# The attention's output stage on TensorE: state products of a tile first, then its value products

## The chip, the cores and the metric

The kernel runs on one core of one Trainium2 chip. The metric is device time in microseconds (us) of one launch: 959.07 us is the median of three runs of the kernel before. One further execution was taken with the hardware profiler; every row below is from that one.

## The reference

Three stages follow one another. The first is a linear attention with a decay per key dimension, over 4 batches, 8 heads, 768 steps and a head dimension of 48:

```python
for t in range(S):
    state = f[:, :, t, :, None] * state + einsum('bhd,bhe->bhde', k[:, :, t], v[:, :, t])
    y[:, :, t] = einsum('bhd,bhde->bhe', q[:, :, t], state)
```

Its output, as 3072 rows of 384, goes through a dense layer (`x @ w_in`, softplus, `@ w_out`, with 2048 hidden columns), and that result through eight experts of 1024 hidden columns. Each expert takes 384 rows, assigned greedily by the gate's logits. All of it is in fp32.

## The kernel before

**The attention in tiles.** The 768 steps of a batch are cut into 6 tiles of 128 steps, 24 tiles in all. `wide_attention(g)` computes one. It brings the keys and queries of all 8 heads into decayed form (`kb`, L363, and `qb`, L367; two heads, a *pair*, share the 128 rows of a PSUM column block), multiplies them to the masked score matrix `A` (L372, L374), carries the state on into the next tile (`kt` by L380, state sum by L386, L393 and L394), and then makes the output `py`. `py` is one PSUM bank of 128 steps x 8 heads x 48 columns.

**The output stage, L396 to L403.** Two kinds of matmul add up in `py`, all in fp32:

- the *state product* of a pair, L399: stationary `qb[:, pr, :]` (128 columns), moving `s_old[:, pr, :]` (96 columns), output on all 128 partitions. A tile has four of them. The first tile of a batch has no old state and leaves them out, so 20 of the 24 tiles have them.
- the *value products*, L402: for each head and each half `z` of the 128 steps the stationary operand is `A[:, h, z]` (64 columns), the moving one is `vn[:, h, :]` (48 columns), and the output is on 64 partitions. A tile has sixteen.

Before the change the four pairs go one after another: the state product of the pair, then the four value products of its two heads. Each state product carries `start=True`; the value products of these tiles carry `start=False` and add to it. In a batch's first tile the value products carry `start=True`.

In the trace each of these fp32 matmuls shows as two records, so a state product is "x2" and the four value products of a pair are "x8".

**What comes after it.** `finish` (L311) copies `py` to `x` on ScalarE (L313), transposes it on TensorE (L320) and splits it into `xh` (L322) and `xl` (L323), the input of the dense layer `moe1`. `moe1(u)` takes three tiles at a time. Per block `fc` of 128 hidden columns it runs nine matmuls into `h` (L558), then ScalarE (L561 to L563), VectorE (L564, L569) and GpSimd (L570, `gl`) make the softplus and split it in two parts, and up to nine matmuls into `acc` use them (L502 and L503 with `gh`, L504 with `gl`).

**What sets the order.** The streams (weights in, attention tiles, dense layer) are merged step by step in `merge`, and a scheduler that simulates the engines' time then fixes the order of instructions on each engine. TensorE executes its list in that order. Code written in another order thus moves the two loops of the output stage, and may also move what the scheduler puts around them, on every engine. From the expert stage on, TensorE's order is written by hand.

In the early part, the weights of the dense layer come as 64-bit numbers and VectorE decodes them to fp32 tiles `w` (L444 to L446); TensorE transposes some of them (L467), ScalarE copies that out (L469, `wT`), and TensorE multiplies it by the gate (L473).

Of the kernel before, what the change touches and what calls it, by code (L numbers as in the profile page):

```python
# [73 lines left out]
def body(ctx, tc, q, k, v, f_logit, w_in, w_out, w_gate, w1, w2, c_mask, c_mat, out, wide):  # L74
    nc = tc.nc
    B, H, S, D = q.shape
    DM = H * D
    NP = H // 2
# [85 lines left out]
    def to_T(x, early=False):  # L164
        p = ps_h.tile([128, NP, 128], F32, name="h") if early else ps_at.tile([128, NP, 128], F32, name="p_at")
        for pr in range(NP):
            nc.tensor.transpose(p[:, pr, :], x[:, 2 * pr:2 * pr + 2, :].rearrange("p a d -> p (a d)"), ident)  # L167
        return p
# [142 lines left out]
    def finish(g, py):  # L311
        x = att.tile([128, DM], F32, name="x", bufs=1)
        nc.scalar.activation(x, py.rearrange("p h d -> p (h d)"), AF.Copy)  # L313
        u, j = divmod(g, TU)
        if j == 0:
            XT[u] = [(xtc() if wide is not None and u > 2 and u % 3 == 1 else xtp).tile([128, DC, TU * 128], F32R, name=n) for n in ("xh", "xl")]
        xh, xl = XT[u]
        px = ps_at.tile([128, DC, 128], F32, name="p_at")
        for c in range(DC):
            nc.tensor.transpose(px[:, c, :], x[:, c * 128:(c + 1) * 128], ident)  # L320
        js = slice(j * 128, (j + 1) * 128)
        nc.scalar.activation(xh[:, :, js], px, AF.Copy)  # L322
        nc.vector.tensor_sub(xl[:, :, js], px, xh[:, :, js].bitcast(F32))  # L323
# [27 lines left out]
    def wide_attention(g):  # L351
        b, i = divmod(g, S // 128)
        first, last = i == 0, i == S // 128 - 1
        qn, kn, vn = loaded.pop(g)
        G, R = decays.pop(g)
        A = AA[g % NF]
        half = (slice(0, 64), slice(64, 128))
        mul = nc.vector.tensor_mul
        pair = lambda x, pr: x[:, 2 * pr:2 * pr + 2, :].rearrange("p a d -> p (a d)")

        pk = to_T(kn, g < GA)
        kb = att.tile([128, NP, 128], F32, name="kb")
        mul(kb, pk, G)  # L363
        yield
        pq = to_T(qn, g < GA)
        qb = att.tile([128, NP, 128], F32, name="qb")
        mul(qb, pq, R)  # L367
        yield
        p = [ps_at.tile([128, NP, 128], F32, name="p_at") for _ in half]
        for pr in range(NP):  # L370
            for z, a in zip(half, p):
                nc.tensor.matmul(a[:, pr, :], kb[z, pr, :], qb[z, pr, :], start=True, stop=True)  # L372
        for r, a in enumerate(p):
            nc.vector.copy_predicated(A[:, r::2], mask[:, 0, None, :].to_broadcast([128, NP, 128]), a)  # L374
            yield
        s_old, s_new = SS[i % 2], SS[(i + 1) % 2]
        if not last:
            pt = ps_at.tile([128, NP, 128], F32, name="p_at")
            for pr in range(NP):
                nc.tensor.transpose(pt[:, pr, :], kb[:, pr, :], ident)  # L380
            kt = att.tile([128, NP, 128], F32, name="kt", bufs=1)
            nc.scalar.activation(kt, pt, AF.Copy)
            yield
            pS = ps_at.tile([128, NP, 2 * D], F32, name="p_at")
            for pr in range(NP):
                nc.tensor.matmul(pS[:, pr, :], kt[:, pr, :], pair(vn, pr), start=True, stop=True)  # L386
            for r in range(2):
                h, c = half[r], slice(D * r, D * r + D)
                end = R[h, :, 127:].to_broadcast([64, NP, D])
                if first:  # L390
                    mul(s_new[h, :, c], pS[h, :, c], end)
                else:
                    nc.vector.tensor_add(s_new[h, :, c], pS[h, :, c], s_old[h, :, c])  # L393
                    nc.gpsimd.tensor_mul(s_new[h, :, c], s_new[h, :, c], end)  # L394
            yield
        py = ps_at.tile([128, H, D], F32, name="p_at")  # L396
        for pr in range(NP):
            if not first:
                nc.tensor.matmul(pair(py, pr), qb[:, pr, :], s_old[:, pr, :], start=True, stop=False, skip_group_check=True)  # L399
            for h in (2 * pr, 2 * pr + 1):  # L400
                for z in half:
                    nc.tensor.matmul(py[z, h, :], A[:, h, z], vn[:, h, :], start=first, stop=True, skip_group_check=True)  # L402
        finish(g, py)  # L403
        yield

# [246 lines left out]
    for g in range(NU * TU):  # L652
        if wide is None:
            streams.append((load_f(g), g * 30.0 - 9.1, 30.0, 1))
            streams.append((load_tile(g), g * 30.0 - 9.0, 30.0, 1))
            streams.append((counted(attention(g), left_t), g * 30.0, 60.0, 26))
        else:
            t = g * TA if g < NA else NA * TA + (g - NA) * TB
            streams.append((load_f(g), t - TF - TA, TA, 1))
            streams.append((decay(g), t - TF, DD, 4))  # L660
            streams.append((load_tile(g), t - TA, TA, 1))
            streams.append((counted(wide_attention(g), left_t), t, TD, 8) + ((AH,) if g < NH else ()))
# [76 lines left out]
    if fast:  # L739
# [4 lines left out]
        first = cst.tile([128, KF], F32, name="first")  # L744
# [551 lines left out]
```

## Time and profile before

| | |
|---|---|
| three runs | 958.22, 959.07 and 961.91 us; median 959.07 us |
| the profiled execution's own time | 963.57 us |
| its span, first to last instruction | 961.8 us |
| TensorE busy | 902.9 us, 94% of the span, 6605 matmul records |
| VectorE, ScalarE, GpSimd busy | 498.0, 469.2 and 480.7 us |
| mean granted TensorE clock | 0.966 of full speed |

The profiled execution is 4.50 us above the median. An engine's busy time is the sum of its instructions' durations with overlaps counted once. Matmuls are pipelined, so one matmul's duration is longer than the distance to the next; the distance from start to start is what a matmul costs in a row of them. In the timeline's rows the first number is the start in us from the span's beginning, the second the time from the first start to the last end of the merged records. A bracket at the end of a row names how long the engine sat idle before it and who released it.

### The profile page before, as it was taken

To read this page: it belongs to the slowest core of one execution; us is meant where nothing else is said; L and a number is where in the kernel's file an instruction comes from. 1 tells how busy PE (TensorE), PEld (TensorE's weight loads), DVE (VectorE), ACT (ScalarE), POOL (GpSimd) and SP (SyncE) were. 2 spreads that over 40 slices of the span, in tenths; PEclk is the share of its full clock that TensorE was granted. 3 is DMA by queue.
4 is the path that set the end of the run, shared out by engine and by line. 5 is a ranking of instruction groups with operands and counts; after the bars stand their busy time and mean duration, and the time that the engine had idled before them with its cause. 6 is when DMAs were issued, how large, how long until landed. Compare 5 with 4: busy or idle time off the path is not lost.

```text
span 961.8 us, 17212 instructions
## 1 busy us (share of the span) xinstructions
PE 902.9 (94%) x6605; PEld 842.6 (88%) x6605; DVE 498.0 (52%) x1275; ACT 469.2 (49%) x959; POOL 480.7 (50%) x500
## 2 busy tenths in 40 slices
PE   3888999999999999999999999999699999999995
PEld 2778999999999999999999998889588889889895
DVE  6886887444445445544553343335465656652320
ACT  3565656455554555555545676733243334335321
POOL 6664665334534344543332443546565676558721
PEclk9977999999999999999999998999799999999898
DMA  9563341122222212222100000003144325427200
GB/s 174 157 172 91 95 119 34 50 42 47 63 42 43 58 36 48 49 56 38 26 25 2 25 1 10 1 17 139 43 157 157 118 88 178 160 66 247 75 26 29
DMA packets 130844, 72.20 MB, mean 75 GB/s; under 512 B 102464, under 2 KB 120256, under 8 KB 130752
## 3 DMA queue, kind: packets, MB, share of 16 engines
q1 hardware_dynamic: 77216, 52.04, 18.6%
q10 hardware_dynamic: 50464, 9.52, 5.8%
q0 software_dynamic: 3072, 9.44, 2.9%
q8 instruction: 54, 0.88, 0.4%
q14 instruction: 38, 0.31, 0.1%
HBM read 61.55 MB, written 9.44 MB: 74 GB/s over the span
## 4 chain that ended last, share of the span: by engine, by line
PE 79%; DVE 6%; issue 6%; ACT 3%; DMA 3%; POOL 3%; SPq 0%; ACTq 0%; POOLq 0%; DVEq 0%
PE h L558 20%; PE h L1170 7%; PE acc L502 7%; PE acc L504 6%; PE acc L503 6%; PE p_at L167 3%; PE p_at L402 3%; PE p_at L399 3%; PE acc L1159 3%; PE p_at L372 2%; PE acc L1161 2%; PE acc L1160 2%; PE p_at L386 2%; PE counts L1012 2%; PE counts L1080 1%
## 5 line engine op out<-in xcount | busy, mean ns | idle before, releaser
L570 POOL TENSOR_TENSOR g<-e,g 128x384 fp32r<-128x384 f32 x128 | 130.3, 1019 | 230.4 <-DVE g L569 223.9
L564 DVE SCALAR_TENSOR_TENSOR e<-h,e 128x384 f32<-128x384 f32 x123 | 68.1, 554 | 148.4 <-ACT e L563 147.8
L558 PE MATMUL h<-xh,wih 128*128 128x384 f32 x369 | 128.8, 350 | 1.5 <-DVE e L564 1.5
L558 PE MATMUL h<-xl,wih 128*128 128x384 f32 x369 | 126.8, 344 | 1.7 <-DVE xl L323 1.7
L558 PE MATMUL h<-xh,wil 128*128 128x384 f32 x369 | 127.0, 344 | 0.0
L561 ACT ACTIVATE e<-h 128x384 f32<-128x384 f32 x123 | 59.7, 486 | 111.8 <-PE h L558 109.4
L502 PE MATMUL acc<-woh,g 128*128 128x392 f32 x304 | 105.7, 351 | 0.6 <-DVE g L569 0.6
L503 PE MATMUL acc<-wol,g 128*128 128x392 f32 x304 | 104.0, 342 | 0.0
L504 PE MATMUL acc<-woh,g 128*128 128x392 f32 x304 | 86.8, 348 | 0.9 <-POOL g L570 0.9
L1123 POOL TENSOR_TENSOR w0l<-wf,w0h 128x512 fp32r<-128x512 f32 x48 | 61.2, 1305 | 43.4 <-ACT w0h L1120 41.0
L1176 ACT ACTIVATE hh<-h 128x384 fp32r<-128x384 f32 x64 | 31.0, 486 | 103.2 <-PE h L1170 98.1
L563 ACT ACTIVATE e<-e,chalf 128x384 f32<-128x384 f32 x128 | 78.6, 614 | 3.3 <-ACT e L562 0.3
L558 PEld LDWEIGHTS h<-xh,wih 128*128 128x128 f32 x369 | 70.5, 191 | 4.3 <-DVE e L564 2.6
L1170 PE MATMUL h<-gxh,w0h 128*128 128x384 f32 x192 | 70.5, 367 | 2.9 <-DVE hl L1177 1.7
L558 PEld LDWEIGHTS h<-xl,wih 128*128 128x128 f32 x369 | 70.8, 192 | 2.2 <-DVE xl L323 2.0
L558 PEld LDWEIGHTS h<-xh,wil 128*128 128x128 f32 x369 | 70.7, 192 | 0.2
L1177 DVE SCALAR_TENSOR_TENSOR hl<-h,hh 128x384 fp32r<-128x384 f32 x64 | 35.5, 555 | 67.1 <-ACT hh L1176 66.8
L1159 PE MATMUL acc<-w1h,hh 128*128 128x384 f32 x192 | 68.2, 355 | 0.0
L562 ACT ACTIVATE e<-e 128x384 f32<-128x384 f32 x128 | 66.8, 523 | 2.8 <-ACT e L561 0.3
L1170 PE MATMUL h<-gxl,w0h 128*128 128x384 f32 x192 | 66.8, 348 | 0.3 <-DVE gxl L1144 0.2
L569 DVE CAST g<-e 128x384 fp32r<-128x384 f32 x128 | 58.0, 455 | 17.3 <-PE acc L549 6.5
L1170 PE MATMUL h<-gxh,w0l 128*128 128x384 f32 x192 | 66.4, 346 | 0.0
(260 smaller groups left out, 2175.8 us busy)
## 6 DMA issues: line engine op xcount, KB each, us to landing
wf<-in_moe_w_dram SPq DMA_DIRECT2D x32, 768.0 KB, 7.2
raw<-in_moe_w_in_dram SPq DMA_DIRECT2D x16, 384.0 KB, 3.2
raw<-in_moe_w_out_dram SPq DMA_DIRECT2D x16, 384.0 KB, 3.1
natf<-in_f_logit_dram SPq DMA_DIRECT2D x24, 192.0 KB, 3.1
natk<-in_k_dram SPq DMA_DIRECT2D x24, 192.0 KB, 3.2
natq<-in_q_dram ACTq DMA_DIRECT2D x24, 192.0 KB, 3.6
vn<-in_v_dram ACTq DMA_DIRECT2D x24, 192.0 KB, 2.8
X<-x SPq DMA_DIRECT2D x24, 192.0 KB, 1.9
```

The lines of the kernel that those rows point to most:

```text
L502: nc.tensor.matmul(a, gh[:, js], woh[:, fc, :a.shape[1]], start=(fc == 0), stop=False)
L503: nc.tensor.matmul(a, gh[:, js], wol[:, fc, :a.shape[1]], start=False, stop=False)
L504: nc.tensor.matmul(a, gl[:, js], woh[:, fc, :a.shape[1]], start=False, stop=(fc == FB - 1))
L558: nc.tensor.matmul(h, w[:, c, fs], x[:, c, :], start=(n == 0), stop=(n == 3 * DC - 1))
L561: nc.scalar.activation(e, h, AF.Abs)
L562: nc.scalar.activation(e, e, AF.Exp, scale=-1.0)
L563: nc.scalar.activation(e, e, AF.Ln, bias=chalf, scale=0.5)
L564: nc.vector.scalar_tensor_tensor(e, h, 0.0, e, op0=OP.max, op1=OP.add)
L570: nc.gpsimd.tensor_sub(gl, e, gh.bitcast(F32))
L1123: nc.gpsimd.tensor_sub(l, src[:, c], h.bitcast(F32))
L1159: nc.tensor.matmul(acc[j], hh[:, js], bh[:, fc, :], start=(fc == 0), stop=False)
L1170: nc.tensor.matmul(h, w[:, c, fs], x[:, c, :], start=(n == 0), stop=(n == 3 * DC - 1))
```

## The change

The two loops are taken apart. All four state products of a tile are issued first, then all sixteen value products. Only the first state product carries `start=True`, the flag that clears the bank; the other three write other columns of the same bank without it. The number of matmuls, their operands and their shapes stay the same.

```diff
         py = ps_at.tile([128, H, D], F32, name="p_at")
-        for pr in range(NP):
-            if not first:
-                nc.tensor.matmul(pair(py, pr), qb[:, pr, :], s_old[:, pr, :], start=True, stop=False, skip_group_check=True)
-            for h in (2 * pr, 2 * pr + 1):
-                for z in half:
-                    nc.tensor.matmul(py[z, h, :], A[:, h, z], vn[:, h, :], start=first, stop=True, skip_group_check=True)
+        if not first:
+            for pr in range(NP):
+                nc.tensor.matmul(pair(py, pr), qb[:, pr, :], s_old[:, pr, :], start=(pr == 0), stop=False, skip_group_check=True)
+        for h in range(H):
+            for z in half:
+                nc.tensor.matmul(py[z, h, :], A[:, h, z], vn[:, h, :], start=first, stop=True, skip_group_check=True)
         finish(g, py)
         yield
```

What the scheduler makes of it stands in TensorE's and VectorE's lists. A tile in the middle of the program, on TensorE (`SS_107` is the old state, `AA_105` the scores, `g_3438` the softplus of one block of the dense layer); three more pairs of rows like the first two, all with a minus, stand right ahead of these:

```order
-L399 MATMUL p_at<-SS_107,qb 128x96
-L402 MATMUL p_at<-vn,AA_105 64x48 x4
-L558 MATMUL h<-xh,wil 128x384
+L399 MATMUL p_at<-SS_107,qb 128x96 x4
+L402 MATMUL p_at<-vn,AA_105 64x48 x16
 L502 MATMUL acc_2776<-woh,g_3438 128x392
 L503 MATMUL acc_2776<-wol,g_3438 128x392
```

The eight alternating rows have become two, and one matmul of the dense layer has moved from behind the block to a place ahead of it. Of the 20 tiles with a state, 16 have exactly these two rows with nothing between. In the first two tiles three L473 matmuls stand among the value products, as they did before; in one later tile three L558 do, and in the last tile dense-layer matmuls do.

Early in the program, on TensorE, where the dense layer's first block begins (`w_738` is a decoded weight tile). Before:

```order
L558 MATMUL h<-xh,wih 128x384
L558 MATMUL h<-xl,wih 128x384
L558 MATMUL h<-xh,wil 128x384
L467 MATMUL p_at<-ident,w_738 128x128 x3
L473 MATMUL p_at<-wg,wT 128x8 x3
L380 MATMUL p_at<-ident,kb 128x128 x4
```

and now:

```order
L372 MATMUL p_at<-qb,kb 128x128 x8
L558 MATMUL h<-xh,wih 128x384 x2
L467 MATMUL p_at<-ident,w_738 128x128 x3
L558 MATMUL h<-xl,wih 128x384
L558 MATMUL h<-xh,wil 128x384
L558 MATMUL h<-xh,wih 128x384
```

The transposes of `w_738` (L467) stood behind all eighteen matmuls of two blocks; now they stand behind the first two of them. On VectorE, the same place:

```order
 L475 TENSOR_TENSOR wol<-acc_719,woh 128x8
-L323 TENSOR_TENSOR xl<-p_at,xh 128x3x128
 L446 SCALAR_TENSOR_TENSOR w_738<-raw,w_738 128x384
+L323 TENSOR_TENSOR xl<-p_at,xh 128x3x128
+L374 COPY_PREDICATED AA_105<-mask,p_at 128x4x128 x2
 L444 TENSOR_SCALAR w_758<-wt 128x384
-L374 COPY_PREDICATED AA_105<-mask,p_at 128x4x128 x2
```

The last step of `w_738` (L446) now comes ahead of `xl` (L323) instead of behind it.

## Rows read from the trace of the kernel before

**Rows 1.** The page: busy times of the engines, and the chain that ended last.

```profile
PE 902.9 (94%) x6605; PEld 842.6 (88%) x6605; DVE 498.0 (52%) x1275; ACT 469.2 (49%) x959; POOL 480.7 (50%) x500
...
PE 79%; DVE 6%; issue 6%; ACT 3%; DMA 3%; POOL 3%; SPq 0%; ACTq 0%; POOLq 0%; DVEq 0%
```

**Rows 2.** Stretches: length; busy PE, PEld, DVE, ACT, POOL (instructions); TensorE clock; DMA; GB/s.

```profile
50.00:90.00 40.00, 34.50 (x209) 31.46 (x210) 29.57 (x60) 22.71 (x52) 22.50 (x24) 0.71 0.51 138
90.00:185.00 95.00, 94.28 (x707) 89.58 (x706) 69.10 (x127) 59.27 (x130) 47.99 (x49) 1.00 0.32 79
185.00:512.00 327.00, 327.00 (x2547) 309.77 (x2547) 159.38 (x329) 167.23 (x320) 136.84 (x150) 1.00 0.21 42
512.00:640.00 128.00, 122.76 (x695) 114.39 (x694) 47.82 (x113) 80.27 (x164) 54.22 (x58) 0.96 0.02 7
```

**Rows 3.** Timeline of TensorE: the output stage of one tile, start, length, what.

```profile
311.93 0.36 PE L399 MATMUL p_at<-SS,qb 128*128 128x96 f32 x2
...
312.59 0.46 PE L399 MATMUL p_at<-SS,qb 128*128 128x96 f32 x2
312.98 0.44 PE L402 MATMUL p_at<-vn,AA 128*64 128x48 f32 x8
313.35 0.46 PE L399 MATMUL p_at<-SS,qb 128*128 128x96 f32 x2
...
314.87 0.44 PE L558 MATMUL h<-xh,wil 128*128 128x384 f32 x1
315.15 0.34 PE L502 MATMUL acc<-woh,g 128*128 128x392 f32 x1
315.32 0.34 PE L503 MATMUL acc<-wol,g 128*128 128x392 f32 x1
```

**Rows 4.** Timeline of TensorE: a batch's first tile, state sum (L386), then value products.

```profile
405.80 1.03 PE L386 MATMUL p_at<-vn,kt 128*128 128x96 f32 x8
406.76 1.14 PE L402 MATMUL p_at<-vn,AA 128*64 128x48 f32 x32
407.83 0.44 PE L558 MATMUL h<-xh,wih 128*128 128x384 f32 x1
```

**Rows 5.** Instructions of L399 and L402: duration ns min/median/max, first and last start.

```profile
L399 PE MATMUL p_at<-SS,qb x160: 243/276/351, 46.2 to 505.5; 128*128 128x96 f32 x160
...
L402 PE MATMUL p_at<-vn,AA x768: 221/222/343, 31.9 to 505.9; 128*64 128x48 f32 x192
```

**Rows 6.** Timeline of TensorE: a tile whose state sum stands right ahead of its output stage.

```profile
486.59 1.03 PE L386 MATMUL p_at<-vn,kt 128*128 128x96 f32 x8
487.46 0.39 PE L399 MATMUL p_at<-SS,qb 128*128 128x96 f32 x2
...
490.42 0.45 PE L502 MATMUL acc<-woh,g 128*128 128x392 f32 x1
```

**Rows 7.** The chain that ended last, in order of time: start, length, what.

```profile
62.93 0.37 PE p_at L402 x8
...
122.77 0.47 issue
...
133.94 1.83 PE h L558 x9
```

**Rows 8.** Timeline, 71 to 80 us: waits of TensorE, and VectorE's last decoding step.

```profile
71.96 0.81 DVE L446 SCALAR_TENSOR_TENSOR w<-raw,w 128x384 int32<-128x384 int32 x1
72.10 0.45 PE L558 MATMUL h<-xl,wih 128*128 128x384 f32 x1 [1.71 <-DVE xl L323]
...
76.55 0.49 PE L467 MATMUL p_at<-ident,w 128*128 128x128 f32 x3
...
79.51 1.33 PE L473 MATMUL p_at<-wg,wT 128*128 128x8 f32 x6 [2.46 <-ACT wT L469]
```

**Rows 9.** The page's costliest groups: busy, mean ns of one, idle before.

```profile
L570 POOL TENSOR_TENSOR g<-e,g 128x384 fp32r<-128x384 f32 x128 | 130.3, 1019 | 230.4 <-DVE g L569 223.9
...
L504 PE MATMUL acc<-woh,g 128*128 128x392 f32 x304 | 86.8, 348 | 0.9 <-POOL g L570 0.9
```

## The prediction

> **What bounds the kernel now.** I read the page first. TensorE is busy for 94% of the span and makes 79% of the chain that ended last; no other engine passes 52% [rows 1]. Since such a share is a mean over stages, I then cut the span into stretches [rows 2]. From 185 to 512 us TensorE is busy for 327.00 of 327.00 us, and from 90 to 185 us for 94.28 of 95.00, both at a granted clock of 1.00, the 2.4 GHz level. In these 422 us nothing but TensorE's own list sets the time, and any us taken off that list moves everything behind it forward. From 50 to 90 us it is different: TensorE is busy for 34.50 of 40 us and the mean clock is 0.71, a mixture of the 2.4 and the 1.2 GHz level. There, what TensorE saves may turn into waiting. The output stage runs in all three stretches, from 46.2 to 505.9 us [rows 5].
>
> Next I looked at the timeline of one tile's output stage [rows 3]. It begins at 311.93 and the next foreign matmul starts at 314.87, so the stage costs 2.94 us. Inside it, a state product (two records) takes 312.98 - 312.59 = 0.39 us from start to start, and the four value products of a pair (eight records) 313.35 - 312.98 = 0.37 us. No wait stands anywhere in it. The question is whether 0.39 and 0.37 are what such matmuls cost, or what the alternation costs.
>
> A batch's first tile answers it, because there the same shapes run unmixed [rows 4]. The state sum L386 has the state product's shape (128 x 128 stationary, 96 moving, fp32): eight records from 405.80 to 406.76, 0.96 us with the turn to the value products in it. With no turn behind it, the same eight take 487.46 - 486.59 = 0.87 us [rows 6]: 0.109 us a record, so two cost 0.22 us, not 0.39. The 32 records of sixteen value products take 407.83 - 406.76 = 1.07 us, or 0.27 us for eight, not 0.37. So each change of the stationary shape, from 128 to 64 columns or back, leaves a gap. A pair has two changes and pays 0.76 - 0.22 - 0.27 = 0.27 us for them.
>
> **The change, part by part.**
>
> *The gaps.* Removed: three of the four alternations of each tile with a state. The count of such tiles is 160 records of L399 / 2 records / 4 pairs = 20 [rows 5]. The new list for a tile, four state products and then sixteen value products, has the shapes and the order of the first tile's row pair, so I price it by that: 0.96 + 1.07 = 2.03 us [rows 4], against 2.94 us [rows 3]. I take 2.94 - 2.03 = 0.91 us for a tile; three pairs of gaps, 3 x 0.27 = 0.81 us, say nearly the same from inside the stage. Where the state sum stands right ahead of the stage, which is so in seven tiles, the stage takes 490.42 - 487.46 = 2.96 us [rows 6]; I take 0.93 us there. One difference is unpriced by these rows: the first tile's value products clear, the new ones accumulate. The row of eight accumulating ones bounds that from above, since 0.37 us for eight contains two changes of shape [rows 3]; without the changes they can't be slower than that, and 4 x 0.37 = 1.48 us in place of 1.07 would leave a gain of 0.50 us a tile. From below nothing speaks for faster ones. I take 1.07, since it is the row of an unbroken run.
>
> *Which tiles count.* The chain that ended last passes through the tile at 62.52 (its value products stand in it at 62.93), and leaves TensorE from 122.77 to 133.94 for a chain over the other engines [rows 7]. So the tile at 125.58, inside that gap, gains nothing for the end: TensorE would only wait longer at 133.94. The tile at 46.15 isn't in the chain either. The other 18 are. That gives 7 x 0.93 + 11 x 0.91 = 16.5 us. If the other engines' cover of those two tiles were not there, 2 x 0.91 = 1.8 us more would be won.
>
> *The flag.* Three clearing flags of a tile vanish. A flag is a bit of an instruction that is issued anyway. I cost it at nothing; in the rows no record differs in a way that would fit a cost for it, and its bounds are inside those of the value products above.
>
> *The rest of TensorE's list.* The scheduler has moved other matmuls too. A change of kind costs its gap there as well: the first L558 behind a block takes 315.15 - 314.87 = 0.28 us against 0.17 us for the next matmul [rows 3]. In the new list there are four fewer places where the dense layer's matmuls follow small ones, 4 x 0.11 = 0.4 us.
>
> *The early part.* The transposes of `w_738` now stand ahead of sixteen matmuls, and `xl` behind the last decoding step. Before, TensorE waited 1.71 us for `xl`; that can grow by the step that now goes ahead, 0.81 us [rows 8]. In return L473, which waited 2.46 us for `wT`, can be served earlier, since `wT` comes from those transposes. The bounds are -0.8 and +2.5 us. As the clock also moves between its levels here and the stretch isn't bound by TensorE, I take 0 and keep the bounds; a clock that stays low longer can eat the same 2.5, so I use 2.5 on both sides.
>
> *Other engines.* They issue what they issued, in slightly other places. DMA issues are the same; early on, the key and the decay load of one tile each go ahead of one weight load on SP's queue, which I count to the early part's bounds. PSUM: `py` is held about 0.9 us less. ScalarE's copy L313 follows the last value product, as before.
>
> The sum is 16.5 + 0.4 = 16.9 us. The profiled execution, 963.57 us with its span of 961.8, would become 946.7. It lies 4.50 us above the median, so I take the sum from the median: 959.07 - 16.9 = **942.2 us**, 1.8% less.
>
> **The rivals.**
>
> *Value products held to their weight loads.* The state products run at 0.109 us a record [rows 6], and if that is the load of 128 columns, one of 64 would take 0.054. Then 32 would cost 1.74 us and not 1.07, the stage 2.70, and 18 tiles would give 18 x 0.24 = 4.3 us: 954.8 us. For it speaks only that 0.109 fits a load. Against it: 1.07 us for 32 [rows 4], and eight accumulating ones in 0.37 us, two changes included, where eight loads alone would be 0.43 [rows 3]. The Trainium skill, page "TensorE: Matmul & The Clock Gate", section "LDWEIGHTS (loading the stationary operand)", states this rule: the load takes the number of columns divided by 1.2, in ns. An estimate by that page's figures is 8 x 107 + 32 x 53 = 2.56 us a tile without any gap; the trace agrees for 128 columns and disagrees for 64. Chance 0.04.
>
> *Half given back.* In the gap from 122.77 to 133.94 the other engines were as tight as TensorE [rows 7]. Were they so at every second tile, nine tiles would count: 9 x 0.91 + 0.4 = 8.6 us, 950.5 us. For it: the 16.5 us come out of 460 us, in which every other engine gets less time. Against: VectorE, the busiest, has 159.38 of 327 us in the long stretch [rows 2]. Chance 0.08.
>
> *Slower: TensorE meets L504 before GpSimd is done.* In the new list L504 often stands right behind L503 of the same accumulator, where matmuls of the next block stood between. L504 needs GpSimd's `gl`, 1019 ns an instruction, and waited only 0.9 us in all before [rows 9]. A late `gl` costs up to 1.02 us; to lose 0.5% (4.8 us) on top of the gain, (16.9 + 4.8) / 1.02, or 21 such waits in full, are needed. For it: the moves are many, among 85 blocks. Against: the scheduler moved L504 behind a simulated time of `gl`, and with the same rule it left two short waits before. It would give 964 us or more. Chance 0.03.
>
> *No difference.* That the change doesn't do what it says is ruled out by the list: 16 of 20 tiles have the two rows unbroken and the others nearly so. What remains is that the gap belongs to something that the new order keeps, such as adding to columns just written. Against: the turn back from value to state products writes other columns and leaves a gap too, since 0.39 and 0.37 are both too long. 959 us, chance 0.02.
>
> **How the numbers follow.** My forecast, 937 to 950, has a chance of 0.83. Its low end is all 20 tiles and the early bound, 16.9 + 1.8 + 2.5 = 21.2 us, or 937.9, and about 1 us for the runs' scatter. Its high end is the upper bound of the value block, 18 x 0.50 + 0.4 = 9.4 us, or 949.7. The range reaches on to the half given back, to 951; the cases above that hold less than 0.1. A measurement of this kernel can tell about 0.5%, 4.8 us, from no change. Faster by more than that: 0.83 + 0.08 = 0.91. Within it: 0.04 + 0.02 = 0.06. Slower: 0.03.
>
> **What would show it.** In the profile after, eight records of L399 should run from start to start of the value products in 0.96 us and 32 of L402 in about 1.07, the stage in 2.0 to 2.1 us. The record count stays 6605 but for lost ones, TensorE's busy time falls by 16 to 18 us, and the last output stage starts some 16 us before 505. The forecast is wrong if the value products stay at 0.37 us for eight, if new idle time of TensorE appears between 90 and 512 us, or if the long stretch gets shorter and a stretch behind it longer.

## The result, and the profile after

The changed kernel takes **943.14 us** (median of four runs, 941.18 to 946.80) against 958.64 us of the kernel before on the same chip (956.42 to 961.91): a ratio of 0.9847, 95% interval 0.9821 to 0.9874, or 15.5 us less. The prediction said 942.2 us, 937 to 951. The profiled execution took 942.85 us with a span of 941.0 us.

The page after, busy times and the chain that ended last, answers to [rows 1]:

```profile
PE 873.9 (93%) x6605; PEld 823.2 (87%) x6605; DVE 500.4 (53%) x1275; ACT 467.3 (50%) x959; POOL 482.9 (51%) x500
...
PE 77%; DVE 7%; issue 6%; ACT 3%; POOL 3%; DMA 3%; ACTq 0%; SPq 0%; POOLq 0%; DVEq 0%
```

The record count is the same and TensorE's busy time is 29.0 us less, while the span of the profiled execution fell by 20.8. So TensorE's idle time rose by 8.2 us, from 961.8 - 902.9 = 58.9 to 941.0 - 873.9 = 67.1. VectorE's share of the chain rises from 6% to 7%; it comes back below.

The same stretches as [rows 2], of the kernel after:

```profile
50.00:90.00 40.00, 34.13 (x238) 31.60 (x239) 33.78 (x63) 24.70 (x55) 25.57 (x27) 0.83 0.52 138
90.00:185.00 95.00, 90.15 (x704) 86.47 (x703) 69.81 (x124) 57.76 (x128) 49.55 (x48) 1.00 0.31 78
185.00:512.00 327.00, 326.98 (x2614) 316.26 (x2611) 161.05 (x340) 174.62 (x336) 139.66 (x153) 1.00 0.21 42
512.00:640.00 128.00, 122.75 (x757) 113.14 (x756) 50.58 (x129) 75.92 (x156) 58.27 (x62) 0.97 0.03 10
```

From 185 to 512 us TensorE is still busy throughout, and 2614 records instead of 2547 fit in. From 90 to 185 us it was busy for 94.28 us and is now busy for 90.15: there it has begun to wait, and 4.1 of the 8.2 us are here.

TensorE's timeline of two output stages after, one with a dense-layer matmul ahead of it, one with the state sum (L386) directly ahead, answers to [rows 3, 6]:

```profile
122.14 1.03 PE L399 MATMUL p_at<-SS,qb 128*128 128x96 f32 x8
123.10 1.14 PE L402 MATMUL p_at<-vn,AA 128*64 128x48 f32 x32
124.17 0.44 PE L558 MATMUL h<-xh,wil 128*128 128x384 f32 x1
...
339.56 1.03 PE L386 MATMUL p_at<-vn,kt 128*128 128x96 f32 x8
340.42 1.06 PE L399 MATMUL p_at<-SS,qb 128*128 128x96 f32 x8
341.41 1.14 PE L402 MATMUL p_at<-vn,AA 128*64 128x48 f32 x32
342.48 0.44 PE L558 MATMUL h<-xl,wih 128*128 128x384 f32 x1
```

The stage takes 124.17 - 122.14 = 2.03 us, of which the state products have 0.96 and the value products 1.07; the other takes 342.48 - 340.42 = 2.06 us. Every unbroken stage of this trace at the 2.4 GHz level lies between 2.02 and 2.06 us.

To see where in the program the time went, I cut every profiled execution at three events that all versions share: the start of the transposes (L320) of the fourth and of the seventh tile, and the start of the matmul at L521, the gate's check behind the attention. The profiled executions of all runs (us; the last column is the span):

```
run             to 4th   4th-7th   7th-check   check-end    span
before          102.66     85.00      325.20       448.9   961.8
e1_oneflag       99.91     85.00      325.20       448.6   958.7
e2_apart        101.08     84.96      325.20       448.7   959.9
after            98.39     85.22      308.80       448.6   941.0
e4_again        101.42     84.23      308.81       450.8   945.3
e11_again2      101.00     84.55      308.94       450.1   944.6
e3_twos         100.07     84.28      312.87       450.1   947.3
e7_late          99.89     85.06      308.79       449.0   942.7
e9_byhalf        96.84     87.01      321.11       448.4   953.4
e5_light_before  89.36     85.80      325.20       444.3   944.7
e6_light_after   89.25     83.43      308.86       454.7   936.2
e8_state64       99.39     83.78      305.84       454.1   943.1
e12_state64b    100.25     83.18      305.78       448.6   937.8
e10_both64       99.46     87.10      301.76       454.7   943.0
```

The third column repeats within 0.15 us for one order, and there the gain stands: 325.20 - 308.80 = 16.4 us, with 15 of the 20 output stages in it. Not all of that is won, since the new list has 18 matmul records behind the check that stood ahead of it. From the same start to the last matmul of L504 each list has the same 3476 records: 484.37 to 484.38 us in the first three rows, 469.89 to 469.97 in the three of the new order (after, e4_again, e11_again2). That is 14.4 us, and so 2 us of the 16.4 only moved. The first and the fourth column scatter by 2 to 3 us from execution to execution, also where the lists are the same, and the second by up to 1 us; a comparison of totals alone tells much less than this column.

### The profile page after: what moved, and what is told of

It is laid out like the page before. It is cut to its first block, busy times and chain, and to the rows that moved or that the text cites. A ratio compares the mean times of both kernels' runs of the same rounds, so it can differ in the third digit from the quotient of the medians.

```text
span 941.0 us, 17206 instructions
## 1 busy us (share of the span) xinstructions
PE 873.9 (93%) x6605; PEld 823.2 (87%) x6605; DVE 500.4 (53%) x1275; ACT 467.3 (50%) x959; POOL 482.9 (51%) x500
## 4 chain that ended last, share of the span: by engine, by line
PE 77%; DVE 7%; issue 6%; ACT 3%; POOL 3%; DMA 3%; ACTq 0%; SPq 0%; POOLq 0%; DVEq 0%
PE h L558 19%; PE h L1170 8%; PE acc L502 7%; PE acc L504 6%; PE acc L503 6%; PE p_at L167 3%; PE acc L1159 3%; PE acc L1161 2%; PE acc L1160 2%; PE p_at L372 2%; PE p_at L402 2%; PE p_at L386 2%; PE counts L1012 2%; PE p_at L399 2%; PE counts L1080 1%
## 5 line engine op out<-in xcount | busy, mean ns | idle before, releaser
L564 DVE SCALAR_TENSOR_TENSOR e<-h,e 128x384 f32<-128x384 f32 x123 | 68.2, 555 | 135.9 <-ACT e L563 135.3
L558 PE MATMUL h<-xh,wih 128*128 128x384 f32 x369 | 127.4, 346 | 7.5 <-DVE e L564 6.7
L558 PE MATMUL h<-xh,wil 128*128 128x384 f32 x369 | 126.2, 342 | 0.0
L558 PE MATMUL h<-xl,wih 128*128 128x384 f32 x369 | 126.2, 342 | 0.0
L502 PE MATMUL acc<-woh,g 128*128 128x392 f32 x304 | 105.3, 350 | 0.6 <-DVE g L569 0.6
L504 PE MATMUL acc<-woh,g 128*128 128x392 f32 x304 | 88.4, 348 | 0.9 <-POOL g L570 0.9
L563 ACT ACTIVATE e<-e,chalf 128x384 f32<-128x384 f32 x128 | 78.6, 614 | 3.6 <-ACT e L562 0.7
L558 PEld LDWEIGHTS h<-xh,wih 128*128 128x128 f32 x369 | 69.8, 189 | 10.8 <-DVE e L564 8.9
L1170 PE MATMUL h<-gxh,w0h 128*128 128x384 f32 x192 | 69.5, 362 | 2.9 <-DVE hl L1177 1.7
L558 PEld LDWEIGHTS h<-xl,wih 128*128 128x128 f32 x369 | 70.2, 190 | 0.2
L558 PEld LDWEIGHTS h<-xh,wil 128*128 128x128 f32 x369 | 70.2, 190 | 0.2
L1170 PE MATMUL h<-gxl,w0h 128*128 128x384 f32 x192 | 66.1, 344 | 0.3 <-DVE gxl L1144 0.3
L1170 PE MATMUL h<-gxh,w0l 128*128 128x384 f32 x192 | 65.9, 343 | 0.0
```

Of the source, the lines that this page charges most:

```text
L502: nc.tensor.matmul(a, gh[:, js], woh[:, fc, :a.shape[1]], start=(fc == 0), stop=False)
L504: nc.tensor.matmul(a, gl[:, js], woh[:, fc, :a.shape[1]], start=False, stop=(fc == FB - 1))
L558: nc.tensor.matmul(h, w[:, c, fs], x[:, c, :], start=(n == 0), stop=(n == 3 * DC - 1))
L563: nc.scalar.activation(e, e, AF.Ln, bias=chalf, scale=0.5)
L564: nc.vector.scalar_tensor_tensor(e, h, 0.0, e, op0=OP.max, op1=OP.add)
L1170: nc.tensor.matmul(h, w[:, c, fs], x[:, c, :], start=(n == 0), stop=(n == 3 * DC - 1))
```

## Experiments

Two questions were put. What makes the gap at each turn: the shape of the stationary operand (my theory), the clearing flag, or adding to columns just written? And why did the tiles ahead of the seventh give so little? A third came up on the way: when do value products run faster than their weight loads?

**e1_oneflag: the flag alone.** The order before, with one clearing flag.

```diff
-nc.tensor.matmul(pair(py, pr), qb[:, pr, :], s_old[:, pr, :], start=True, stop=False, skip_group_check=True)
+nc.tensor.matmul(pair(py, pr), qb[:, pr, :], s_old[:, pr, :], start=(pr == 0), stop=False, skip_group_check=True)
```

> The order of before, state product and its four value products pair by pair, with the clearing flag on the first state product alone; every engine's list reads as before's. Shape theory (the gap belongs to each change between stationary operands of 128 and of 64 columns): nothing changes, the stage stays at 2.94 us a tile and the ratio to before is 0.997 to 1.003. Flag theory (the gap belongs to the three clearing flags that went away): the stage falls to 2.0 to 2.5 us and the ratio to 0.985 to 0.992. As its list is before's, its early part also shows how far the clock and the first 90 us scatter from run to run: the third x transpose began at 68.22 us in before and at 66.04 us in the changed kernel.

Measured: 960.15 us, ratio 1.0 (0.9978 to 1.0022). TensorE's timeline of one stage of this kernel:

```profile
198.58 0.35 PE L399 MATMUL p_at<-SS,qb 128*128 128x96 f32 x2
198.87 0.44 PE L402 MATMUL p_at<-vn,AA 128*64 128x48 f32 x8
...
201.15 0.44 PE L402 MATMUL p_at<-vn,AA 128*64 128x48 f32 x8
201.51 0.44 PE L558 MATMUL h<-xl,wih 128*128 128x384 f32 x1
```

201.51 - 198.58 = 2.93 us, as before. The flag costs nothing, and the third column is unchanged to the hundredth.

**e2_apart: alternating, but never onto fresh columns.** The value products behind each state product are those of the pair two further on. As in e1_oneflag, the first state product alone carries the flag.

```diff
...
-            for h in (2 * pr, 2 * pr + 1):
+            for h in (2 * ((pr + 2) % NP), 2 * ((pr + 2) % NP) + 1):
```

> Still alternating, with as many changes of shape as before and the same lists, but each state product is followed by the value products of the pair two further on, so that no matmul adds to columns that the matmuls right ahead of it wrote. Shape theory: the stage stays at 2.94 us, the ratio at 0.997 to 1.003. Write theory (the gap is a wait for columns just written): the turn from a state product to the value products loses its gap, the stage falls to 2.0 to 2.5 us and the ratio to 0.985 to 0.993.

Measured: 960.16 us, ratio 0.9995 (0.9976 to 1.0014). Its stage, the first row and the row behind it:

```profile
199.70 0.36 PE L399 MATMUL p_at<-SS,qb 128*128 128x96 f32 x2
...
202.64 0.44 PE L558 MATMUL h<-xl,wih 128*128 128x384 f32 x1
```

2.94 us: which columns were written last makes no difference. Both rivals fall; the alternation of shapes remains.

**e3_twos: half of the turns taken out.** Two state products, their value products, and once more.

```diff
-        for pr in range(NP):
-            if not first:
+        for i in range(0, NP, 2):
+            for pr in () if first else (i, i + 1):
...
-            for h in (2 * pr, 2 * pr + 1):
+            for h in range(2 * i, 2 * i + 4):
```

> Two state products, the eight value products of their pairs, and the same once more: three changes of shape inside a tile where before had seven and the changed kernel has one. Shape theory, 0.91 us over six changes or 0.15 us a change: the stage takes 2.03 + 2 x 0.15 = 2.33 us, 0.61 us less than before; 18 tiles give 11 us, ratio 0.986 to 0.992. Write theory: hardly a value product follows its own state product, the stage takes about 2.0 us, as the changed kernel's.

Measured: 948.56 us, ratio 0.9885 (0.9868 to 0.9901). One stage:

```profile
198.01 0.58 PE L399 MATMUL p_at<-SS,qb 128*128 128x96 f32 x4
198.52 0.67 PE L402 MATMUL p_at<-vn,AA 128*64 128x48 f32 x16
199.13 0.69 PE L399 MATMUL p_at<-SS,qb 128*128 128x96 f32 x4
199.74 0.67 PE L402 MATMUL p_at<-vn,AA 128*64 128x48 f32 x16
200.34 0.44 PE L558 MATMUL h<-xl,wih 128*128 128x384 f32 x1
```

2.33 us. Against the new order's 2.03 it has two changes of shape more, 0.15 us each; the order before has six more, (2.94 - 2.03) / 6 = 0.15 us each. The cost goes with the number of changes and with nothing else that was varied. Since changes come in pairs, from 128 columns to 64 and back, 0.15 us is the mean of both directions.

**e4_again: the new order on that chip.**

> The changed kernel once more. The stage takes 2.02 to 2.06 us. If the 4 us by which its profile was ahead at 99 us come from the order, they come back: the transposes of x in the fourth tile begin at 98 to 99 us. If they come from when the clock rose, the value products of the first tile (1.07 us there, 1.88 us in before) and that start scatter by 2 to 4 us.

Measured: 946.28 us, ratio 0.9862 (0.9846 to 0.9879), stages 2.02 to 2.06 us. The fourth tile's transposes begin at 101.42 us and the first tile's value products take 1.88 us, so the lead of the first 99 us did not come back.

**e5_light_before and e6_light_after: is it VectorE that takes the rest?** In the new order TensorE waits between 90 and 185 us where it hardly did before. The waits for `e` by what ended them, this stretch, first of the kernel before, then of the kernel after (in all, times, longest):

```profile
PE h L558 <- DVE e L564: 0.7, 2, 0.5
```

```profile
PE h L558 <- DVE e L564: 4.5, 4, 2.2
```

The longest of them, 2.17 us, stands ahead of the fourth tile's transposes, behind the first output stage of this stretch; the next, 1.09 us at 130.48, behind the second one. Both come back in e4_again (2.16 and 1.09 us) and in e11_again2 (2.14 and 1.10). The chain that ended last, of the kernel after, shows what is in front of the longest:

```profile
90.40 1.33 DVE w L444
...
91.75 0.57 DVE w L445
...
92.35 1.61 DVE w L446
...
93.98 0.47 ACT woh L462
94.45 0.56 ACT e L563
...
95.04 0.57 DVE e L564
```

VectorE decodes a block of the dense layer's weights (L444 to L446), ScalarE's copy of it (L462) stands ahead of the softplus step L563, and only behind L564, which reads `h`, does L558 write the next one, at 95.65. In front of the wait at 130.48 the chain has the same three steps (124.56 to 128.79), a copy on ScalarE (L454), L563 and L564. So I took the last decoding step away, once in each order.

```diff
-        stt(m, lo_w, 29, m, op0=OP.logical_shift_right, op1=OP.bitwise_or)
+        pass
```

Both kernels leave out the lowest three mantissa bits of the dense layer's weights.

> The order of before, with VectorE's last decoding step of the dense layer's weights left out (L446, the lowest three mantissa bits): 32 steps of about 0.55 us less for VectorE, 18 us in all, in the first 160 us. It is the base for the next run. Both theories: 3 to 8 us faster than before, since the first 90 us hang on VectorE in part; TensorE's waits for e (L564) between 90 and 185 us stay under 1 us.

> The same leaving-out in the changed order. Theory: in the full kernels the saving of the three tiles between 90 and 185 us is given back because VectorE's decoding keeps e (L564) late: TensorE waited 4.5 and 3.7 us for it there in two runs of the changed kernel, 0.7 us in before's order. With the decoding lighter, those waits fall to 0 to 1.5 us and the distance from the fourth to the seventh x transpose becomes 2 to 3 us shorter than in the run before this one; the time falls by 15 to 17.5 us against it. Rival (the list of TensorE itself has moved, so that it meets e too early whatever VectorE does): waits of 3 us and more stay, the distance differs by under 1 us, the time falls by 13 to 15 us.

Measured: 951.39 us in the order before, ratio 0.9926 (0.9902 to 0.9950); 936.76 us in the new order, ratio 0.9724 (0.9649 to 0.9798). TensorE's waits for `e` from 82 to 175 us, which holds the fourth to the seventh tile in these runs, of e5_light_before and then of e6_light_after:

```profile
PE h L558 <- DVE e L564: 0.9, 2, 0.5
```

```profile
PE h L558 <- DVE e L564: 0.7, 2, 0.5
```

With the step gone the new order waits no more than the other, and from the fourth to the seventh tile it now is 85.80 - 83.43 = 2.37 us shorter, where the kernel after was 0.22 us longer than before. So with less decoding these tiles' gain comes back, in one profiled execution of each kernel. The pair doesn't isolate VectorE's load alone: without the step the scheduler orders the early lists anew, and in TensorE's some 300 of 6605 places differ between e6_light_after and the kernel after. The totals differ by 14.6 us, which is what the rival had said, and don't show it: what was won ahead was lost behind the check (454.7 us in the table, with one wait of 3.8 us of L1017 for `rc`).

**e7_late: the new order from the second batch on.** The first batch's tiles keep the alternation.

```diff
-        for pr in range(NP):
-            if not first:
...
+        for i in range(0, NP, step := NP if g >= S // 128 else 1):
+            for pr in () if first else range(i, i + step):
...
```

> The new order in the tiles of batches 2 to 4 alone (15 tiles with a state); batch 1 keeps the order of before, and so do all lists up to there. Theory (the five tiles of batch 1 give nothing for the end): the time is the changed kernel's within 1.5 us, ratio to before 0.9835 to 0.9875. Rival (all tiles count alike): a quarter of the gain is missing, 3.5 to 4.5 us, ratio 0.988 to 0.990.

Measured: 947.73 us (944.02, 944.51, 950.96 and 954.38), ratio 0.9886 (0.9809 to 0.9964): too wide to tell from the new order or from a cost of 4 us; the median lies where the rival had it. The profiled execution has the seventh tile at 184.95 us and 308.79 us behind it, so the 15 later tiles alone give the 16.4 us of the third column, whatever the first batch does. With the first batch in the old order no wait for `e` over 0.5 us stands between 82 and 188 us. What the first batch's tiles give to the end stays open.

**e9_byhalf: when does a weight load limit value products?** All eight value products of the first half of the steps, then all eight of the second.

```diff
-        for h in range(H):
-            for z in half:
+        for z in half:
+            for h in range(H):
```

> The changed kernel with the value products in another order: all eight of the first half of the steps, then all eight of the second, so that neighbours no longer take turns between the two halves of the array's columns. Load theory (a load of 64 columns costs 0.054 us, and the 0.033 us a record of the value products come from two halves loaded beside one another): 32 records take about 1.75 us in place of 1.07, the stage 2.7 us, and the gain over before shrinks to 3 to 6 us, ratio 0.993 to 0.997. Rival (a small matmul costs 0.033 us whatever its neighbours are): 1.07 and 2.03 us as in the changed kernel, ratio 0.983 to 0.988.

Measured: 956.64 us, ratio 0.9995 (0.9963 to 1.0026). One stage:

```profile
197.52 1.03 PE L399 MATMUL p_at<-SS,qb 128*128 128x96 f32 x8
198.47 1.87 PE L402 MATMUL p_at<-vn,AA 128*64 128x48 f32 x32
200.28 0.44 PE L558 MATMUL h<-xl,wih 128*128 128x384 f32 x1
```

The same 32 records, with the same shapes and operands, take 200.28 - 198.47 = 1.81 us, 0.056 us a record instead of 1.07 / 32 = 0.033. They only no longer take turns between the two halves of 64 columns. The stage is 2.76 us, the third column keeps 4.1 us of its gain of 16.4 (up to the last L504, 2.7 of 14.4), and the total can't be told from before, though 3 to 6 us had been expected. In the kernel after these records start in twos, 0.006 us apart, and the next two 0.058 us behind; here one starts every 0.058 us, but for a short stretch where the halves meet.

**e8_state64, e12_state64b and e10_both64: taking the last changes out.** If a change costs 0.15 us and products of 64 columns that take turns run at 0.033 us, the state products too can be cut into two halves of 64 columns. In e10_both64 the state sum is cut as well; it computes only the blocks of its output that are used.

```diff
-            for pr in range(NP):
-                nc.tensor.matmul(pair(py, pr), qb[:, pr, :], s_old[:, pr, :], start=(pr == 0), stop=False, skip_group_check=True)
+            for pr, z in itertools.product(range(NP), half):
+                nc.tensor.matmul(pair(py, pr)[z], qb[:, pr, z], s_old[:, pr, :], start=(pr == 0), stop=False, skip_group_check=True)
```

and, in e10_both64 alone:

```diff
-            for pr in range(NP):
-                nc.tensor.matmul(pS[:, pr, :], kt[:, pr, :], pair(vn, pr), start=True, stop=True)
+            for pr, r in itertools.product(range(NP), range(2)):
+                nc.tensor.matmul(pS[half[r], pr, D * r:D * r + D], kt[:, pr, half[r]], vn[:, 2 * pr + r, :], start=True, stop=True)
```

> New order, and each state product cut in two halves of 64 stationary columns, so that the whole stage has one stationary shape (eight state products of 64 columns instead of four of 128). Shape theory: the change inside the tile goes too (0.1 to 0.15 us), and if halves load beside one another as the value products' do (0.033 us a record), 16 records take 0.53 us in place of 0.87: the stage takes 1.55 to 1.65 us, and 15 tiles give 6 us more, ratio to before 0.977 to 0.981. If 64 columns cost half of 128 here, 0.054 us a record, the stage takes 1.9 us and the ratio is 0.982 to 0.986.

> The new order, with the state products (L399) in two halves of 64 columns as in the run with halved state products, and the state sum (L386) cut the same way: eight products of 64 stationary and 48 moving columns, where there were four of 128 and 96. Shape theory (a change between 128 and 64 stationary columns costs about 0.15 us, and 64-column products that take turns between the two column halves cost 0.033 us a record): L386 runs in about 0.53 us instead of 0.87, and where L399 follows it directly no change of shape stands between them. From the seventh tile's transposes to the gate's check that is some 17 times 0.3, or 4 to 6 us less than 305.8, so 300 to 302 us. If nothing behind that stretch gives it back, the time is some 4 us below the halved state products alone and 7 us below the new order, ratio about 0.976. Rival (the end is set behind that stretch by the clock's low stretches and the expert stage, as the halved state products showed): the stretch gets shorter as said, and the total stays within 2 us of the new order, ratio 0.983 to 0.987. Second rival (loads): L386 stays at 0.87 us, and nothing moves.

> The new order once more, on the chip of the runs beside it, so that all three stand against the same runs of the kernel before. Expected: ratio 0.984 to 0.987, stage 2.02 to 2.06 us, 308.8 us from the seventh tile's transposes to the gate's check. If it should lie within 1 us of both kernels with halved products, the halving brings nothing that a measurement can tell; if it lies 3 us or more above them, what the halving takes from TensorE's list reaches the end.

> The new order with the state products in two halves of 64 columns, once more, with more runs. Stretch: 305.8 us from the seventh tile's transposes to the gate's check, stage 1.73 us. Theory that TensorE's list sets the end: 3 us below the new order beside it, ratio about 0.981. Rival (clock phases and the expert stage decide): no difference from the new order beyond 1 us, as the first such run had it.

Measured: e8_state64 944.61 us, ratio 0.9836 (0.9774 to 0.9899). Then, beside each other, e11_again2 943.33 us, 0.9823 (0.9780 to 0.9867); e12_state64b 941.45 us, 0.9815 (0.9768 to 0.9862); e10_both64 943.68 us, 0.9819 (0.9768 to 0.9870). Two stages of e12_state64b, the second with L386 directly ahead, then a tile of e10_both64:

```profile
197.20 0.88 PE L399 MATMUL p_at<-SS,qb 128*64 128x96 f32 x16
197.91 1.09 PE L402 MATMUL p_at<-vn,AA 128*64 128x48 f32 x32
198.93 0.44 PE L558 MATMUL h<-xl,wih 128*128 128x384 f32 x1
...
337.60 1.03 PE L386 MATMUL p_at<-vn,kt 128*128 128x96 f32 x8
338.56 0.88 PE L399 MATMUL p_at<-SS,qb 128*64 128x96 f32 x16
```

```profile
339.63 0.67 PE L386 MATMUL p_at<-vn,kt 128*64 128x48 f32 x16
340.13 0.85 PE L399 MATMUL p_at<-SS,qb 128*64 128x96 f32 x16
340.80 1.09 PE L402 MATMUL p_at<-vn,AA 128*64 128x48 f32 x32
341.82 0.44 PE L558 MATMUL h<-xl,wih 128*128 128x384 f32 x1
```

The stage is 1.73 us, less than 1.9 and more than the 1.55 to 1.65 that were expected if halved state products ran at 0.033 us a record: 16 of them take 0.67 us in e10_both64, with no change ahead of them, which is 0.042 a record. In e10_both64, L386 to the end of the stage is 341.82 - 339.63 = 2.19 us, where it is 2.92 us in the kernel after (339.56 to 342.48).

The turns bear out the shape theory once more. From the start of the last state product to that of the first value product it is 0.205 us in the kernel after and 0.076 in e12_state64b, where both have 64 stationary columns, though the moving ones still go from 96 to 48. In its place L386, still with 128 columns, takes 338.56 - 337.60 = 0.96 us up to L399, where it takes 340.42 - 339.56 = 0.86 us in the kernel after. The gap went where the change of the stationary width went. The number of output partitions goes with that width in all these rows, and no run parts the two.

The third column falls as expected, to 305.8 and to 301.8 us, 7 us below the new order. The total doesn't follow, as the rival had it: the three kernels lie within 2.3 us of each other with overlapping intervals. In e10_both64's execution 2.6 us are lost from the fourth to the seventh tile (87.10 against 84.55 us in e11_again2) and 4.6 us behind the check (454.7 against 450.1). The expert stage, from the first to the last L1170, of e11_again2 and then of e10_both64, with the columns of the stretches above, and under the second a wait in it:

```profile
667.70:928.00 260.30, 252.00 (x1912) 233.32 (x1913) 129.87 (x474) 97.20 (x208) 154.59 (x145) 0.97 0.35 118
```

```profile
658.60:926.80 268.20, 254.40 (x1913) 235.48 (x1914) 133.93 (x474) 97.59 (x208) 155.33 (x145) 0.96 0.34 114
...
PE counts L1017 <- DVE rc L1014: 4.2, 2, 3.9
```

It starts 9.1 us earlier and ends 1.2 us earlier. One wait of 3.9 us for VectorE's `rc` and a slightly lower clock make most of that; the same wait stood in e6_light_after, the other run that came early to this stage. Behind the check e8_state64 lost nearly as much (454.1 us in the table) with waits for `rc` of 1.0 us in all, at a clock of 0.96 in the expert stage, and e12_state64b, the same kernel, lost nothing (448.6 us) at 0.99. So halving is no proven gain over the change, and what sets the length of the expert stage in an execution stays open.

## Why the prediction was right, and where it was off

*The gaps* were right in place, mechanism and size: 2.94 us was to become 2.03 and became 2.02 to 2.06. That a change of the stationary shape makes the gap is now shown by runs, since neither the flag (e1) nor the columns written (e2) matter, the loss follows the number of changes (e3), and the gap moves with them (e12). In the stretch with 15 tiles, the time from each start of L399 or L402 to the next start on TensorE sums to 46.32 us before and 32.96 after, 13.4 us less; the terms for these 15 tiles were 13.8.

*The value products* were priced by a row in which they clear, 1.07 us for 32, with 1.48 as the bound. They take 1.07 us while accumulating.

*The flag at nothing* was right (e1).

*Fewer exits, 0.4 us*, can be seen in the same sums: 586 matmuls of L558 take 106.8 us from start to start before, 577 take 104.8 after. At the old mean 577 would take 105.2, so 0.4 us were won. The other 1.6 us, and 1.3 us of L502 to L504, are the 18 matmuls that only moved behind the check. They make nearly all of the difference between the 16.4 us by which the third column fell and the 13.4 of the stages, and 2 us of it come back by the last L504. The 14.4 us up to there stand against 13.8 + 0.4 = 14.2 us in the terms of the sum.

*Which tiles count* was the step that failed, in part. I counted 18 tiles as on the chain, since TensorE was busy for 94.28 of 95 us from 90 to 185 us [rows 2]. For two of the three tiles there, at 94.46 and 137.62 us in the kernel before, that was 1.8 us of gain. But a busy TensorE does not say how near behind it the others are: with 0.9 us less work at each tile it met VectorE's `e`, and its waits for it grew from 0.7 to 4.5 us in the kernel after. The output stage of the first of the three stands ahead of the fourth tile's transposes, where executions scatter too much to tell what it gave, but a wait of 2.17 us follows it, more than the 0.9 that it saves. The other two stand between these transposes and the seventh's. Their stages got 1.8 us shorter, and I had counted one of them, 0.9 us; the three executions of the new order took 84.23 to 85.22 us there, against 84.96 to 85.00: 0.3 us of gain in the mean. The chain, e5 and e6 point to what holds `e` back, the decoding. This is the rival of the half that is given back, but at two or three tiles and not at nine. It was visible, as the chain there already left TensorE once [rows 7]; I used that for the one tile in the gap and not for its neighbours.

*The early part at 0, within 2.5 us* held as far as it can be told. From 50 to 90 us TensorE's waits of over 0.5 us sum to 5.5 us before and 6.5 after. The fourth tile comes at 99.91 to 102.66 us in the order before and at 98.39 to 101.42 in the new one, so the executions of one order differ by more than the orders.

*The signs.* The stage, the rows and the record count came out as said. TensorE's busy time was to fall by 16 to 18 us and fell by 29.0; 10.0 of it lie ahead of the fourth tile's transposes (77.10 to 67.15 us), where the idle time rose by 5.7 us in these two executions. And new idle time of TensorE between 90 and 512 us, which was to speak against the forecast, did appear: the 4.1 us above.

*The rivals.* "Value products held to their weight loads" was wrong for this order and right for another one, e9. "TensorE meets L504 too early" did not happen: L504's idle time is 0.9 us before and after. "No difference" is out.

The sum of 16.9 us thus was about 1.5 us too large for the 15.5 us beside it; the repeats gave 13.5 us (e4) and 15.8 us (e11). That 943.14 lies 0.9 us from 942.2 is in part the luck of the runs, since repeats of one kernel differ by more.

## What to carry to other kernels

When small matmuls with stationary operands of different widths alternate, look for the same shapes in an unmixed row of the same trace: the difference is the price of the turns, and sorting by shape takes it away. But keep neighbours of 64 columns taking turns between the two halves, since sorting those too costs more than it brings. And count a gain on the busiest engine only as far as the next engine lets it. A stretch where that engine is 99% busy may have a second one right behind it, which its waits and the chain show and the busy share doesn't.

## What the runs showed of the hardware that was not expected

- **A change between 128 and 64 stationary columns costs 0.15 us** at the 2.4 GHz level, the same for two, four and eight changes in a stage, whatever is cleared or written. The Trainium skill, page "TensorEngine Tiling (Array Packing)", section "Key Properties", says that changing the tiling mode drains the engine. The trace agrees in so far as each change costs 0.15 us; whether ordinary matmuls of 128 and 64 columns are two such modes, and whether the gap is a drain, no run here shows.
- **Products of 64 columns run beside their neighbour when the two halves take turns**: 0.033 us a record, against 0.056 where one half follows itself (e9). The same section of the Trainium skill says that different tiles can load weights and multiply in parallel, which agrees. The figure of the Trainium skill's page "TensorE: Matmul & The Clock Gate", section "LDWEIGHTS (loading the stationary operand)", 64 / 1.2 = 53 ns by an estimate, agrees with the second case and not with the first.
- **The first 100 us and the expert stage differ between executions of one program.** The mean granted clock of the first 90 us was 0.87 in the kernel before and 0.91 in e1_oneflag, whose instructions stand in the same order on every engine; the fourth tile came at 102.66 and at 99.91 us. Later the expert stage had a mean clock of 0.96 in one execution of the kernel with halved state products and 0.99 in another, and took 264.2 and 257.3 us. Several us of a total are decided there, more than some of the changes tried here are worth.
